# Sigmoid attention into a swish MoE layer: values loaded ahead of group 2, group 0's values between the first half visits, keys cast and turned tile by tile

## Chip, cores, metric

The kernel runs on 1 core of one Trainium2 chip. The metric is device time in microseconds (us); less is better. A core has TensorE (PE, its weight loads shown as PEld), VectorE (DVE), ScalarE (ACT), GpSimd (POOL) and SyncE (SP); POOL and SP issue DMAs here.

## What is computed

```python
scores = q @ k.transpose(0, 1, 3, 2) / sqrt(64) - log(448)      # 8 batches, 12 heads, 448 x 64
attn_out = sigmoid(scores) @ v
x = attn_out.transpose(0, 2, 1, 3).reshape(8 * 448, 12 * 64)    # 3584 x 768
h = x @ w_in                                                     # 768 x 2048
out = (h * sigmoid(beta * h)) @ w_out                            # 2048 x 768
```

Inputs and output are float32; the kernel works in float16 with float32 sums.

## The kernel before

Heads are taken four at a time: a **group** `g` holds the queries and keys of 4 heads of a batch, with 32 partitions for each head, and a batch has 3 groups (`QPB`). A group has two **slots** of 2 heads. 448 keys are three tiles of 128 (`JF` = 3) and a last tile of 64.

Loads go through POOL's queue (`load_one` L111, `load_v` L132, `load_w_in` L151, `load_w_out` L158) and cast float32 to float16 on the way. Only what is needed first goes another way: half of group 0's queries and all its keys are brought in as float32 by SP (L723, "staged" in a piece of `gt`) and cast by ACT and DVE (L747 to L750). `transpose` (L191) turns queries and keys 32 by 32 on DVE; keys of a group take one instruction for the three full tiles (L204) and one for the last (L208). `load_v` brings the full tiles with four DMAs (L136) and the last tile with two (L143); `double_v_last` (L145) copies the last tile's values to a second half of the partitions, on DVE.

`score` (L215) is a matmul of a key tile with queries into a PSUM score tile; `weigh` (L227) is the sigmoid on ACT that reads it (L230). For the start of batch 0 there are three score tiles and two further PSUM banks (L711), and the work is cut into **half visits** (`half_visit`, L256): half of the queries (224) of a group, first with key tiles 0 and 1, then with tile 2 and the last. Each uses two score tiles and ends in two ACT instructions. `attend` (L279) multiplies the weights with v into two PSUM banks (L291), which DVE copies to `xT` (L300). Then the first layer starts: `first_half(n)` makes n `dense1` (L305) of six matmuls on `w_in` each (L171, through the helper `dense`).

All of this is in an order written by hand (`tc.manual_schedule`, L713): each engine takes its instructions in the order of the program. From L713 to L809 the order is written out; behind it `follow(STEPS)` (L810) goes through a long list. The order around the change, before:

1. SP stages; PE runs 11 matmuls on zeros (`idle_units`, L738, L744); group 0's queries and keys are cast and turned.
2. POOL issues, in this order: half the queries and the keys of groups 1 and 2, v of batch 0 (6 DMAs), late queries of groups 0 and 1, `w_in` in 8 pieces, with group 2's late queries between.
3. Six half visits (groups 0, 1, 2, early queries), with 4, 4, 4, 4 and 2 idle units behind the first five (L767 to L771).
4. `double_v_last(0)`, group 0's late queries, `attend(0)`, half visit, `attend(1)`, half visit (L772 to L777), then the others' late queries, `attend(2)` in two parts, and the turning of beta.
5. The score tiles go from three to two, and the first layer starts (L794 to L796); its first matmul waits for the last ACT of the half visits.

The DMA semaphores of POOL are eight in turn; an issue waits for the landing of the eighth issue before it.

Of the kernel before, what the change touches and what calls it, by code (L numbers as in the profile page):

```python
# [8 lines left out]
FP32 = mybir.dt.float32  # L9
FP16 = mybir.dt.float16  # L10
# [3 lines left out]
def kernel(  # L14
# [10 lines left out]
    nc = tc.nc  # L25
# [82 lines left out]
    raws = {}  # L108
# [20 lines left out]
    def last_base(s: int) -> int:  # L129
        return (s % 2 ^ swapped(s // 2)) * KL  # L130

    def load_v(b: int):  # L132
        vs[b] = vp.tile([P, H, JF + 1, D], FP16, tag="v16", name="v16")
        rows = v[b].rearrange("h (p c) d -> p h (c d)", c=NB)
        for i in range(HQ):
            nc.gpsimd.dma_start(  # L136
                out=vs[b][i * BLK : (i + 1) * BLK, :, 0:JF].rearrange("p h j d -> p h (j d)"),
                in_=rows[:, :, JF * i * D : JF * (i + 1) * D],
            )
        rows = v[b].rearrange("h (p c) d -> p h c d", c=NB)  # L140
        for c in range(NF, NB):
            lo = (c - NF) * BLK
            nc.gpsimd.dma_start(out=vs[b][lo : lo + BLK, :, JF], in_=rows[:, :, c])  # L143

    def double_v_last(b: int):  # L145
        nc.vector.tensor_copy(out=vs[b][KL:P, :, JF], in_=vs[b][0:KL, :, JF])
# [44 lines left out]
    def transpose(g: int, r: int, c0: int = 0, c1: int = NB):  # L191
        raw = raws[g][:, r]
        if r == 0:
            if g not in qT:
                qT[g] = qTp.tile([P, NB * BLK, PAIR], FP16, tag="qT", name="qT")
            nc.vector.transpose(
                out=in_order(g // QPB, qT[g][:, c0 * BLK : c1 * BLK]),
                in_=raw[:, c0:c1].rearrange("p c d -> p (c d)").bitcast(FP32),
            )
            return  # L200
        kT[g] = kTp.tile([P, S, PAIR], FP16, tag="kT", name="kT")
        to = kT[g].rearrange("p k e -> p (k e)").bitcast(FP32)
        frm = raw.rearrange("p c d -> p (c d)").bitcast(FP32).rearrange("p (c f) -> p c f", c=NB)
        nc.vector.transpose(  # L204
            out=to[:, 0 : JF * P].rearrange("p (j i q) -> p i j q", j=JF, i=HQ),
            in_=frm[:, 0:NF].rearrange("p (i j) f -> p i j f", j=JF),
        )
        nc.vector.transpose(  # L208
            out=to[:, JF * P :], in_=frm[:, NF:].rearrange("p c f -> p (c f)")
        )  # L210
# [502 lines left out]
    with tc.manual_schedule():  # L713
        raws[0] = rawp.tile([P, 2, NB, D], FP16, tag="raw", name="raw")
        wide = gt.rearrange("p a b -> p (a b)").bitcast(FP32)
        cut = NH * D
        early = [(0, 0, NH), (1, 0, NB)]
        staged = {}
        at = 0
        for r, c0, c1 in early:  # L720
            staged[r] = wide[:, at : at + (c1 - c0) * D]
            at += (c1 - c0) * D
            nc.sync.dma_start(  # L723
                out=staged[r],
                in_=(q, k)[r][0, 0:HQ].rearrange("h (p c) d -> (h p) (c d)", c=NB)[
                    :, c0 * D : c1 * D
                ],
            )
        nc.gpsimd.memset(dummy, 0.0)
        nc.scalar.activation(out=dummy, in_=dummy, func=AF.Sigmoid, bias=0.0, scale=1.0)  # L730

        still = gt[:, NDC - 1, 0:512]
        nc.vector.memset(still, 0.0)
        beta_in = sigp.tile([P, S], FP32, tag="sg", name="beta_in")[0:BLK, 0:P]
        nc.vector.memset(beta_in, 0.0)
        idle = bank("idle_ps", 512)

        def idle_units(n: int, cols: int = 512):  # L738
            for _ in range(n):
                nc.tensor.matmul(  # L740
                    idle[:, 0:cols], still[:, 0:P], still[:, 0:cols], start=True, stop=True
                )

        idle_units(10)  # L744
        idle_units(1, 256)
        raw = raws[0].rearrange("p r c d -> p r (c d)")
        nc.vector.tensor_copy(out=raw[:, 0, 0:cut], in_=staged[0])  # L747
        transpose(0, 0, 0, NH)
        nc.scalar.copy(out=raw[:, 1, cut:], in_=staged[1][:, cut:])  # L749
        nc.vector.tensor_copy(out=raw[:, 1, 0:cut], in_=staged[1][:, 0:cut])  # L750
        transpose(0, 1)
        for g in range(1, QPB):
            load_one(g, 0, 0, NH)
            load_one(g, 1)
        load_v(0)
        nc.sync.dma_start(out=beta_in[0:NDC], in_=moe_beta.rearrange("(c p) -> c p", p=P))
        for g in range(QPB - 1):
            load_one(g, 0, NH, NB)
        for c in range(WCH):
            if c == WCH // 2:  # L760
                load_one(QPB - 1, 0, NH, NB)
            load_w_in(c)
        for g in range(1, QPB):
            transpose(g, 0, 0, NH)
            transpose(g, 1)

        for g in range(QPB):  # L767
            for second in range(2):
                half_visit(g, 0, second)
                if 2 * g + second < 2 * QPB - 1:  # L770
                    idle_units(4 if g < QPB - 1 else 2)  # L771
        double_v_last(0)  # L772
        transpose(0, 0, NH, NB)
        attend(0, 0, QH)
        half_visit(0, QH, 0)
        attend(1, 0, QH)
        half_visit(0, QH, 1)  # L777
        for g in range(1, QPB - 1):
            transpose(g, 0, NH, NB)
        attend(2, 0, QH, (0,))  # L780
        attend(2, 0, QH, (1,))
        for i in range(P // BLK):
            part = slice(i * BLK, (i + 1) * BLK)
            nc.vector.transpose(out=beta_sb[part], in_=beta_in[:, part])
# [24 lines left out]
        first_half(1)  # L809
        follow(STEPS)  # L810
# [30 lines left out]
```

## Time and profile before

| | |
|---|---|
| median of 3 runs | 368.48 us (368.26 to 369.42) |
| the profiled execution | 368.51 us, its span 366.7 us, granted clock 1.0 |
| busy: PE / DVE / ACT / POOL | 361.6 / 271.7 / 248.7 / 154.3 us |
| stretch 0 to 6.00 us, PE busy | 4.67 (idle matmuls on zeros) |
| 6.00 to 13.08, PE / ACT busy | 7.08 / 6.13 |
| 13.08 to 19.42, PE / ACT busy | 5.95 / 6.14 |
| 19.42 to 34.50, PE / ACT busy | 15.08 / 11.89 |
| moved by DMA in these four stretches | 166, 179, 184, 201 GB/s |

The profile is of one execution on the chip, times from the start of its span. A timeline line gives start, length, engine, line of the kernel, operation, what is written and read with shape and type, how many were merged, and in brackets how long the engine had been idle and what ended that. A line of the chain gives start, length and who held the chain. A line of the DMA issues gives what is written and read, queue, count, KB each and the time from issue to landing.

### The profile page before, as it was taken

Reading aid. Unit: us, or ns where it says so; the run is one execution under the profiler, and the core shown is the slowest. Engines: PE = TensorE matmul, PEld = TensorE weight load, DVE = VectorE, ACT = ScalarE, POOL = GpSimd, SP = SyncE. Lnnn points to the kernel's source line nnn. Section 1 sums busy time; section 2 is a strip of 40 time slices with the busy share of each in tenths; the row PEclk is TensorE's granted clock in tenths of the full one; section 3 lists DMA queues with packets and bytes.
Section 4 is the critical chain, followed back from the end, with each engine's and each line's share of the span. In section 5 each row is a group of like instructions: output and inputs, shape, how many; then the busy total and the mean of one; then the engine's idle time right before and its main releaser. Section 6 shows DMA issues by size and latency. Waiting matters only on the chain.

```text
span 366.7 us, 9126 instructions
## 1 busy us (share of the span) xinstructions
PE 361.6 (99%) x3677; PEld 238.0 (65%) x3677; DVE 271.7 (74%) x521; ACT 248.7 (68%) x409; POOL 154.3 (42%) x192
## 2 busy tenths in 40 slices
PE   8999999999999999999999999999999999999996
PEld 3478754457465685557857667666856687679763
DVE  3356569889995796876778678868878667678764
ACT  4987976789765797657865579977874859226410
POOL 7834523504413873117761445841630316316610
PEclk9999999999999999999999999999999999999999
DMA  8999999930363790416919363373303030030234
GB/s 168 184 197 201 199 206 198 236 39 2 50 139 52 160 152 2 74 64 111 156 13 149 52 137 52 49 81 89 52 1 89 2 88 2 0 88 0 56 68 138
DMA packets 42698, 34.76 MB, mean 95 GB/s; under 512 B 21904, under 2 KB 39200, under 8 KB 42656
## 3 DMA queue, kind: packets, MB, share of 16 engines
q0 software_dynamic: 36688, 22.47, 44.8%
q1 hardware_dynamic: 5968, 11.71, 11.5%
q8 instruction: 29, 0.48, 0.6%
q14 instruction: 13, 0.11, 0.1%
HBM read 45.62 MB, written 11.01 MB: 154 GB/s over the span
## 4 chain that ended last, share of the span: by engine, by line
PE 93%; DMA 3%; ACT 2%; DVE 1%; SPq 0%; issue 0%; ACTq 0%; DVEq 0%
PE m_ps L171 71%; PE sco L218 12%; PE av_ps L291 9%; DMA out_dram<-osb 2%; ACT attnT L230 1%; PE idle_ps L740 1%; DMA gt<-in_k_dram 1%; DVE osb L372 0%; SPq L602 0%; ACT osb L425 0%; DVE xT L300 0%; DVE kT L204 0%; ACT raw L749 0%; ACT osb L463 0%; SPq L723 0%
## 5 line engine op out<-in xcount | busy, mean ns | idle before, releaser
L230 ACT ACTIVATE attnT<-sco 128x896 f16<-128x896 f32 (+1 forms) x163 | 139.2, 908 | 37.8 <-PE sco L218 37.1
L372 DVE TENSOR_TENSOR osb<-m_ps,osb 128x448 f32<-128x448 f32 (+2 forms) x197 | 116.3, 596 | 51.1 <-PE m_ps L171 42.0
L171 PEld LDWEIGHTS <-w_in 128*128 128x128 f16 (+1 forms) x948 | 81.0, 100 | 18.8 <-issue 11.0
L171 PE MATMUL m_ps<-xT,w_in 128*128 128x224 f16 (+3 forms) x750 | 85.5, 266 | 0.3 <-ACT attnT L230 0.2
L492 POOL TENSOR_TENSOR gt<-osb,sg 128x448 f16<-128x448 f32 x26 | 29.5, 1135 | 117.8 <-ACT sg L425 107.7
L502 POOL TENSOR_TENSOR gt<-osb,sg 128x448 f16<-128x448 f32 x52 | 58.3, 1138 | 35.1 <-ACT sg L425 33.5
L425 ACT ACTIVATE sg<-osb,beta_sb 128x224 f32<-128x224 f32 (+1 forms) x104 | 54.0, 575 | 10.3 <-DVE osb L372 10.0
L171 PEld LDWEIGHTS <-sum 128*128 128x128 f16 (+1 forms) x444 | 39.9, 99 | 27.4 <-issue 3.6
L171 PEld LDWEIGHTS <-gt 128*128 128x128 f16 (+1 forms) x474 | 36.9, 102 | 25.7 <-issue 7.5
L171 PE MATMUL m_ps<-w_out,gt 128*128 128x384 f16 (+2 forms) x350 | 52.6, 324 | 0.0
L218 PE MATMUL sco<-qT,kT 32*128 32x448 f16 (+3 forms) x864 | 51.5, 340 | 0.3 <-ACT attnT L230 0.2
L171 PEld LDWEIGHTS <-w_S 128*128 128x128 f16 (+1 forms) x486 | 43.9, 99 | 7.0 <-issue 6.0
L171 PE MATMUL m_ps<-w_out,sum 128*128 128x384 f16 (+1 forms) x228 | 40.6, 327 | 0.0
L171 PE MATMUL m_ps<-w_T,sum 128*128 128x384 f16 (+1 forms) x216 | 40.3, 326 | 0.0
L300 DVE CAST xT<-av_ps 128x448 f16<-128x448 f32 (+1 forms) x54 | 28.4, 566 | 14.2 <-PE av_ps L291 14.1
L291 PE MATMUL av_ps<-attnT,v 128*64 128x448 f16 (+3 forms) x400 | 38.2, 343 | 0.0
L171 PE MATMUL m_ps<-xs,w_S 128*128 128x224 f16 (+1 forms) x330 | 36.2, 259 | 0.0
L291 PEld LDWEIGHTS <-v 128*64 128x64 f16 (+1 forms) x432 | 20.4, 108 | 17.7 <-issue 9.8
L425 ACT ACTIVATE osb<-m_ps,beta_sb 128x224 f32<-128x224 f32 x52 | 20.4, 448 | 15.4 <-PE m_ps L171 15.1
L218 PEld LDWEIGHTS <-kT 32*128 32x128 f16 (+1 forms) x864 | 13.5, 96 | 23.1 <-issue 21.5
L320 DVE TENSOR_TENSOR gt<-m_ps,sg 128x224 f16<-128x224 f32 (+1 forms) x40 | 16.6, 434 | 12.5 <-ACT sg L317 12.2
L463 ACT COPY osb<-m_ps 128x448 f32<-128x448 f32 x26 | 13.8, 535 | 17.7 <-PE m_ps L171 15.5
(50 smaller groups left out, 303.5 us busy)
## 6 DMA issues: line engine op xcount, KB each, us to landing
out_dram<-osb SPq DMA_DIRECT2D x100, 96.0 KB, 2.4
raw<-in_k_dram POOLq DMA_DIRECT2D x23, 224.0 KB, 5.7
raw<-in_q_dram POOLq DMA_DIRECT2D x21, 224.0 KB, 4.4
v<-in_v_dram POOLq DMA_DIRECT2D x32, 144.0 KB, 7.0
w_in<-in_moe_w_in_dram POOLq DMA_DIRECT2D x8, 384.0 KB, 10.3
w_out<-in_moe_w_out_dram POOLq DMA_DIRECT2D x4, 768.0 KB, 13.1
v<-in_v_dram POOLq DMA_DIRECT2D x16, 48.0 KB, 6.4
out_dram<-osb SPq DMA_DIRECT2D x4, 192.0 KB, 2.4
```

Source lines behind the costliest of these rows:

```text
L171: nc.tensor.matmul(to[c : c + step], hidden[:, c : c + step], weights, **({} if step == P else {"tile_position": (0, c)}), **flags,)
L218: nc.tensor.matmul(sco[base : base + nk, hh, u0 : u0 + n], kT[g][lo : lo + BLK, jt * P : jt * P + nk, e], qT[g][lo : lo + BLK, c0 : c0 + n ...
L230: nc.scalar.activation(out=at[:, :, 0:n], in_=sco[:, :, 0:n], func=AF.Sigmoid, bias=NEG_LOG_S, scale=MSCALE,)
L291: nc.tensor.matmul(av[hh * D : (hh + 1) * D, 0:n], vs[b][base : base + nk, 2 * (s % NPAIR) + hh, jt], at[base : base + nk, hh, 0:n], start ...
L300: nc.vector.tensor_copy(out=xTs[b][:, s % NPAIR, c0 : c0 + n], in_=av[:, 0:n])
L320: nc.vector.tensor_tensor(out=gt[:, dc, off : off + n], in0=m1[:, 0:n], in1=sg[:, 0:n], op=ALU.mult)
L372: nc.vector.tensor_tensor(out=out, in0=in0, in1=in1, op=op)
L425: nc.scalar.activation(out=out, in_=in_, func=AF.Sigmoid, bias=0.0, scale=beta_sb[:, dc : dc + 1])
L463: nc.scalar.copy(out=oa[:, 0], in_=m)
L492: nc.gpsimd.tensor_tensor(out=gt[:, 2 * d : 2 * d + 2, off : off + QH], in0=ob[:, 0], in1=sg, op=ALU.mult)
L502: nc.gpsimd.tensor_tensor(out=gt[:, dc, off : off + S].rearrange("p (h n) -> p h n", h=2), in0=oa[:, :, j], in1=sg, op=ALU.mult,)
L740: nc.tensor.matmul(idle[:, 0:cols], still[:, 0:P], still[:, 0:cols], start=True, stop=True)
```

## The change

Three things, all in the hand-written start. `load_v` is split into `load_v_full` (the full tiles, of some heads) and `load_v_last` (the last tile, all heads); for batch 0 the last tile of all heads and the full tiles of heads 0 to 3 (group 0's) are issued between group 1's and group 2's queries and keys, and heads 4 to 11 behind them: 10 DMAs instead of 6. Group 0's keys are cast by tile (tile 1 and the last on ACT, tiles 0 and 2 on DVE) and turned by tile. `double_v_last(0)` and `attend(0)` go between the half visits of the early queries, `attend(1)` ahead of group 0's late half visits, and the idle units become 3, 4, 4, 4, 0, 1, with 10 instead of 11 at the start; each call of `idle_units` takes a bank of its own.

```diff
+    def load_v_full(b: int, h0: int, h1: int):
+        rows = v[b, h0:h1].rearrange("h (p c) d -> p h (c d)", c=NB)
         for i in range(HQ):
             nc.gpsimd.dma_start(
-                out=vs[b][i * BLK : (i + 1) * BLK, :, 0:JF].rearrange("p h j d -> p h (j d)"),
+                out=vs[b][i * BLK : (i + 1) * BLK, h0:h1, 0:JF].rearrange("p h j d -> p h (j d)"),
                 in_=rows[:, :, JF * i * D : JF * (i + 1) * D],
             )
+
+    def load_v_last(b: int):
         rows = v[b].rearrange("h (p c) d -> p h c d", c=NB)
         for c in range(NF, NB):
             lo = (c - NF) * BLK
             nc.gpsimd.dma_start(out=vs[b][lo : lo + BLK, :, JF], in_=rows[:, :, c])
...
-        idle_units(10)
+        idle_units(9)
         idle_units(1, 256)
...
-        nc.scalar.copy(out=raw[:, 1, cut:], in_=staged[1][:, cut:])
-        nc.vector.tensor_copy(out=raw[:, 1, 0:cut], in_=staged[1][:, 0:cut])
-        transpose(0, 1)
+        whole = [
+            t[:, 0 : NF * D].rearrange("p (i j d) -> p i j d", j=JF, d=D)
+            for t in (staged[1], raw[:, 1])
+        ]
...
+        def key_cast(copy, j: int):
+            copy(out=whole[1][:, :, j], in_=whole[0][:, :, j])
+
+        def key_turn(j: int):
+            nc.vector.transpose(
+                out=words[:, j * P : (j + 1) * P].rearrange("p (i q) -> p i q", i=HQ),
+                in_=raws[0][:, 1, 0:NF]
+                .rearrange("p c d -> p (c d)")
+                .bitcast(FP32)
+                .rearrange("p (i j q) -> p i j q", i=HQ, j=JF)[:, :, j],
+            )
+
+        key_cast(nc.scalar.copy, 1)
+        nc.scalar.copy(out=raw[:, 1, NF * D :], in_=staged[1][:, NF * D :])
+        key_cast(nc.vector.tensor_copy, 0)
+        key_turn(0)
+        key_turn(1)
+        key_cast(nc.vector.tensor_copy, 2)
+        key_turn(2)
+        nc.vector.transpose(out=words[:, JF * P :], in_=raw[:, 1, NF * D :].bitcast(FP32))
...
         for g in range(1, QPB):
             load_one(g, 0, 0, NH)
             load_one(g, 1)
-        load_v(0)
+            if g == 1:
+                load_v_last(0)
+                load_v_full(0, 0, HQ)
+        load_v_full(0, HQ, H)
...
-        for g in range(QPB):
-            for second in range(2):
-                half_visit(g, 0, second)
-                if 2 * g + second < 2 * QPB - 1:
-                    idle_units(4 if g < QPB - 1 else 2)
         double_v_last(0)
+        for n in range(2 * QPB):
+            half_visit(n // 2, 0, n % 2)
+            if n == 2 * QPB - 2:
+                attend(0, 0, QH)
+            else:
+                idle_units((3, 4, 4, 4, 0, 1)[n])
         transpose(0, 0, NH, NB)
-        attend(0, 0, QH)
+        attend(1, 0, QH)
         half_visit(0, QH, 0)
-        attend(1, 0, QH)
         half_visit(0, QH, 1)
```

More of the change, by code (lines that the diff above doesn't have):

```diff
@@ L130, in last_base @@
         return (s % 2 ^ swapped(s // 2)) * KL
-    def load_v(b: int):
-        vs[b] = vp.tile([P, H, JF + 1, D], FP16, tag="v16", name="v16")
-        rows = v[b].rearrange("h (p c) d -> p h (c d)", c=NB)
+    def load_v_full(b: int, h0: int, h1: int):
+        rows = v[b, h0:h1].rearrange("h (p c) d -> p h (c d)", c=NB)
         for i in range(HQ):
             nc.gpsimd.dma_start(
-                out=vs[b][i * BLK : (i + 1) * BLK, :, 0:JF].rearrange("p h j d -> p h (j d)"),
+                out=vs[b][i * BLK : (i + 1) * BLK, h0:h1, 0:JF].rearrange("p h j d -> p h (j d)"),
                 in_=rows[:, :, JF * i * D : JF * (i + 1) * D],
             )
+    def load_v_last(b: int):
         rows = v[b].rearrange("h (p c) d -> p h c d", c=NB)
@@ L143, in load_v @@
             nc.gpsimd.dma_start(out=vs[b][lo : lo + BLK, :, JF], in_=rows[:, :, c])
+    def load_v(b: int):
+        vs[b] = vp.tile([P, H, JF + 1, D], FP16, tag="v16", name="v16")
+        load_v_full(b, 0, H)
+        load_v_last(b)
     def double_v_last(b: int):
@@ L735 @@
         nc.vector.memset(beta_in, 0.0)
-        idle = bank("idle_ps", 512)
         def idle_units(n: int, cols: int = 512):
+            idle = bank("idle_ps", 512)
             for _ in range(n):
@@ L748 @@
         transpose(0, 0, 0, NH)
-        nc.scalar.copy(out=raw[:, 1, cut:], in_=staged[1][:, cut:])
-        nc.vector.tensor_copy(out=raw[:, 1, 0:cut], in_=staged[1][:, 0:cut])
-        transpose(0, 1)
+        whole = [
+            t[:, 0 : NF * D].rearrange("p (i j d) -> p i j d", j=JF, d=D)
+            for t in (staged[1], raw[:, 1])
+        ]
+        kT[0] = kTp.tile([P, S, PAIR], FP16, tag="kT", name="kT")
+        words = kT[0].rearrange("p k e -> p (k e)").bitcast(FP32)
+        def key_cast(copy, j: int):
[16 more added lines that the diff above has]
+        nc.vector.transpose(out=words[:, JF * P :], in_=raw[:, 1, NF * D :].bitcast(FP32))
+        vs[0] = vp.tile([P, H, JF + 1, D], FP16, tag="v16", name="v16")
         for g in range(1, QPB):
```

## The prediction

> **What bounds the kernel now.** I read the page first: its span, the shares of the engines and the chain that ended last.
>
> ```profile
> span 366.7 us, 9126 instructions
> PE 361.6 (99%) x3677; PEld 238.0 (65%) x3677; DVE 271.7 (74%) x521; ACT 248.7 (68%) x409; POOL 154.3 (42%) x192
> PE 93%; DMA 3%; ACT 2%; DVE 1%; SPq 0%; issue 0%; ACTq 0%; DVEq 0%
> ```
>
> PE is the bound almost everywhere, and behind 19.42 us every engine has the same instructions in the same order in both kernels. So the change is worth what it moves the first dense matmul at 19.42, as far as the stage behind it can follow. That stage I read in the chain in order of time, up to that matmul:
>
> ```profile
> 1.18 3.56 DMA gt<-in_k_dram
> ...
> 6.00 0.62 PE sco L218 x16
> ...
> 16.29 3.08 ACT attnT L230 x4
> ...
> 19.42 2.46 PE m_ps L171 x24
> ```
>
> Columns are start, length, who. The staged keys land at 4.74, are cast and turned, PE scores at 6.00, and the dense stage starts when the last ACT of the block ends. Whether ACT or PE sets the pace in between I read from ACT's timeline:
>
> ```profile
> 6.66 6.28 ACT L230 ACTIVATE early<-sco 128x896 f16<-128x896 f32 x8 [1.33 <-PE sco L218]
> 13.08 6.29 ACT L230 ACTIVATE attnT<-sco 128x896 f16<-128x896 f32 x8
> 20.49 1.87 ACT L317 ACTIVATE sg<-m_ps,beta_sb 128x224 f32<-128x224 f32 x4 [1.12 <-DVE beta_sb L784]
> ```
>
> Sixteen sigmoids run from 6.66 to 19.37 with 0.14 between the eights: 12.71 us. Asked in narrow windows they start at 6.66, 7.47, 8.37, ..., 16.29, 17.11, 18.01. With three score tiles the second tile of a half visit waits for the ACT two back, and that half visit's last matmul starts the ACT after: third = end of the first (7.57) + 0.8 = 8.37; thirteenth = end of the eleventh (15.71) + 0.58 = 16.29. So the block is a **locked chain of PE and ACT**: it moves as a whole with its first ACT, and the idle matmuls only fill PE's waits. DVE's timeline gives the keys:
>
> ```profile
> 4.76 0.39 DVE L750 CAST raw<-gt 128x448 f16<-128x448 f32 x1 [0.51 <-DMA gt<-in_k_dram]
> 5.36 0.58 DVE L204 STREAM_TRANSPOSE kT<-raw 128x384 f32<-128x384 f32 x1 [0.20 <-ACT raw L749]
> 5.86 0.20 DVE L208 STREAM_TRANSPOSE kT<-raw 128x64 f32<-128x64 f32 x1
> 7.46 0.58 DVE L204 STREAM_TRANSPOSE kT<-raw 128x384 f32<-128x384 f32 x1 [1.10 <-DMA raw<-in_k_dram]
> 9.18 0.58 DVE L204 STREAM_TRANSPOSE kT<-raw 128x384 f32<-128x384 f32 x1 [0.67 <-DMA raw<-in_k_dram]
> 14.15 0.35 DVE L146 COPY v<-v 64x768 f16<-64x768 f16 x1 [4.27 <-DMA v<-in_v_dram]
> ```
>
> Group 1's keys land at about 7.43, group 2's at 9.15, the last of v at 14.06: DVE waits on each.
>
> **Keys tile by tile: gain 0.43.** Now the scores wait for a whole ACT half (0.57) and a turn of 384 (0.58). In the changed list the first turn of 128 waits for DVE's cast of tile 0 and also for ACT's cast of tile 1, though it reads tile 0 alone. That ACT copy has 256 columns instead of 448. ACT rows: 0.56 for 448, 0.45 for a 224-column sigmoid, so about 0.45. The turn: 0.20 for 64, 0.58 for 384, on the line between them 0.28 for 128. Turn starts 4.76+0.45+0.03 = 5.24, ends 5.52, PE starts 5.57 (0.05 later, as 5.94 to 6.00) instead of 6.00: 0.43. Bounds: cast 0.45 to 0.57 and turn 0.20 to 0.41 (the 224 row) give 0.18 to 0.51; should the stride slow both casts, nothing is gained, and that is the lower end. Turn 1 ends at 5.72, ahead of the ninth matmul (5.57+0.25). Tile 2 and the tail end by 6.45, while the second half visit comes at 6.85; ACT's extra copy (128 columns) ends by 5.6, ahead of the first sigmoid at 6.23. Two extra turns and a cast on DVE lie before group 1's keys (7.43). They cost nothing on that cover; without it, some 0.3.
>
> **PE's clock: loss 0.1.** The eleven idle matmuls before 6.00 take 4.66, starting 0.43 apart; those at 6.55 take 1.04 for four, 0.22 apart. PE changes from half to full speed at about 6. Scores that start at 5.57 fall partly into the slow time; whole it would cost 0.58 (the undisturbed sixteen at 21.81 take 0.58, at half speed twice that), for the first third of it I take 0.1, 0 to 0.58. The Trainium skill ("TensorE: Matmul & The Clock Gate", Part 1) says the gate opens after a busy window of about 3.4 us that runs freely, so that the switch differs from run to run. One trace can't show that; by it the cost varies between executions and isn't fixed at 6.
>
> **attend(0) between the half visits, attend(1) ahead of the next: loss 0.2.** Of the 29 idle units 26 stay. attend(0) takes 0.91 (14.67 to 15.58, next weight load). Between first and second half visit of group 2 PE has 13.06 to 14.05, of which 0.5 are idle units: it fits, no loss. Between the second and the next score PE had exactly attend(0), 0.91; now one idle unit (0.24) and attend(1) (0.91): 1.15. So the thirteenth ACT comes 0.2 later than its lock, and the last with it. Afterwards PE has nothing between two half visits, 0.7 idle, and both parts of attend(2) come late as before, 0.92 in all, done before the last ACT. Bounds 0 to 0.35 (should the idle unit wait out both DVE casts, 0.69 from the end of attend(0), it is still covered by the 0.7 of scores between).
>
> **v ahead of group 2's queries and keys: nothing lost, barely.** Ahead go two transfers of 48 KB for the last keys and four of 48 KB: 288 KB. The 16 engines move 179 GB/s in 6.00 to 13.08, so 1.65 us. Group 2's keys then land at 9.15+1.65 = 10.8, up to 11.4 if v's last rows lag (landing 12.71 to 14.06 for 96 KB: 1.35 where 0.55 is the rate). They are turned 0.63 later: 11.4 to 12.05. The half visit wants them at 12.43-0.43 = 12.0. Issue: POOL has eight landings outstanding at most: its tenth issue, now one of v, waits for the second to land, group 1's keys.
>
> ```profile
> 7.72 0.61 POOL L143 DMA_DIRECT2D v<-in_v_dram  x1 [1.07 <-DMA raw<-in_k_dram]
> ```
>
>  So group 2's keys are issued at 7.72 instead of 3.03. In this row from issue to landing
>
> ```profile
> raw<-in_k_dram POOLq DMA_DIRECT2D x1, 224.0 KB, 6.1
> ```
>
> most is queueing; in a quiet time (94 us) the same takes 4.2, and as large a transfer with nothing ahead of it (93 us) 3.7: landing by 11.4 then. Cost 0 to 0.05, at the row's 6.1 far more (rival). POOL issues four more DMAs, 0.62 each = 2.5, so the weights of the first layer are issued near 12 instead of 10.29; queued bytes cover that, as w_in's first chunk takes 6.2 to land, its own 2.0 included. The doubling copy stands on DVE behind group 2's turn and takes 0.35 (to 12.4); attend(0) needs it only for its last four matmuls after 12.6. Group 0's late queries, 14.54 now, are wanted at 15.4.
> The Trainium skill ("DMA: Bandwidth & Descriptors", Rules for kernel authors) says to join transfers, as under 64 KB one pays mostly overhead; it speaks against this cut. Here queued transfers of v of 144 KB and of 48 KB follow each other by 0.85 and 0.36, so the trace bears it out little: behind others overhead is hidden. With the fixed cost of about 2.0 us that the page gives (Anatomy of one DMA), an estimate by that page alone is 6 x 2.0 = 12 us more if nothing overlapped, keys at 21.
>
> **Sum.** 0.43 - 0.1 - 0.2 = 0.13 of gain at 19.42. Behind it PE can follow: the w_in chunks land at least 0.5 ahead of their first matmul (last at 31.50 for 32.09), w_out 0.6 (43.62 for 44.21). The profiled execution took 368.51 (span 366.7, 1.8 around it), beside a median of 368.48: 368.51-0.13 = **368.4**. With all good ends 0.51: 368.0; with all bad ones (0, 0.58, 0.35): 369.4.
>
> **Rivals.**
> 1. Group 2's keys come late (slower). For it: issued 4.69 later, behind a landing; all data of this time were waited for. Against: the rate. With the queued 6.1, landing is 13.85, the half visit starts 14.5 instead of 12.0: 368.4+2.5 = 370.9. It decides from a landing beyond 11.4, and from about 12.6 the kernel is over 0.3% slower. Chance 0.14. The Trainium skill's rule on small transfers stands on this side.
> 2. PE's clock opens late, after the first scores and three idle units: 0.58 and 3 x 0.21, less the idle unit that was dropped (0.22): 1.0 lost, 369.3. For: the scores start earlier. Against: 4.4 us of idle matmuls lie before, and before is open to the same. Chance 0.10.
> 3. The gain is real, but w_in lands later by the four issues, and PE waits there instead: 368.5 to 368.9 (0.5 late at the chunks with 0.5 to spare). For: the page's slices stay near 200 GB/s up to 73 us. Against: same bytes. Chance 0.10.
> 4. What no row shows: 0.07, of which 0.04 faster.
>
> My forecast has 0.59. **Chances:** within 0.3% (about 1.1 us, what a measurement of this kernel can tell from no change) 0.59+0.10+0.10 = 0.79; slower 0.14+0.03 = 0.17; faster 0.04, as no case reaches it. Range 367.8 to 369.6: forecast and rivals 2 and 3, and the first part of 1.
>
> **What would show it.** First score at about 5.57; its first ACT 6.23; group 2's first half visit at 12.0 without a wait for DVE or keys; a PE gap of 0.7 before the last half visit of the block; first dense matmul at 19.3; no PE wait for w_in. I am wrong if group 2's turn waits beyond 11.4, if the first turn starts before ACT's cast ends, or if idle matmuls 0.43 apart stand behind the first scores.

## The result, and the profile after

| | before | after |
|---|---|---|
| median, measured side by side | 368.69 us (368.11 to 371.01, 7 runs) | 370.50 us (370.12 to 372.49, 7 runs) |
| profiled execution, span | 368.51, 366.7 | 370.74, 368.8 |

The ratio is 1.0051, 95% interval 1.0029 to 1.0073: slower by about 1.8 us, where 368.4 was forecast. The page of after, the lines that answer to those of before:

```profile
PE 360.9 (98%) x3674; PEld 237.2 (64%) x3674; DVE 272.4 (74%) x524; ACT 249.0 (68%) x410; POOL 156.2 (42%) x196
...
PE 86%; DMA 10%; POOL 2%; issue 1%; DVE 0%; ACT 0%; DVEq 0%; POOLq 0%
```

PE does the same work (360.9), but transfers now hold 10% of the chain instead of 3%, and POOL, which was not on it, 2%. Where they stand shows the chain in order of time, cut at 60 us (start, length, who):

```profile
1.98 5.30 DMA raw<-in_k_dram
...
7.56 0.55 POOL raw L115
...
13.13 9.55 DMA w_in<-in_moe_w_in_dram
22.97 12.85 DMA raw<-in_k_dram
...
36.94 8.98 DMA w_out<-in_moe_w_out_dram
```

The chain no longer goes through the scores. It goes from the landing of group 1's keys to POOL, which issues group 2's keys only then, through POOL's issues to the third piece of the first layer's weights, whose landing at 22.69 lets POOL issue again, and so on to the weights of the second layer, which land at 45.92. So up to there the chain runs through POOL's eight places. PE's timeline around 22 to 25 us, before and then after:

```profile
22.32 1.90 PE L171 MATMUL m_ps<-xT,w_in 128*128 128x224 f16 x18
```

```profile
22.73 1.32 PE L177 MATMUL m_ps<-xT,w_in 128*128 128x224 f16 x12
24.74 0.46 PE L177 MATMUL m_ps<-xT,w_in 128*128 128x224 f16 x3 [0.68 <-DMA w_in<-in_moe_w_in_dram]
```

PE waits 0.68 for the fourth piece of the weights, a wait that the forecast said would not be there. ACT's timeline has the block of half visits (6.10 to 19.61 us):

```profile
6.10 6.28 ACT L236 ACTIVATE early<-sco 128x896 f16<-128x896 f32 x8 [0.82 <-PE sco L224]
12.77 3.06 ACT L236 ACTIVATE attnT<-sco 128x896 f16<-128x896 f32 x4 [0.40 <-PE sco L224]
16.54 3.07 ACT L236 ACTIVATE attnT<-sco 128x896 f16<-128x896 f32 x4 [0.70 <-PE sco L224]
```

ACT has the same instructions in both kernels behind 6 us, so one can set the two traces beside each other instruction by instruction. After minus before: -0.56 at the first sigmoid, -0.31 at the ninth, +0.25 at the thirteenth (16.54 for 16.29), then flat until the first layer; +0.83 and +1.15 at the two instructions that before started at 24.69 and 25.02 (the waits for the weights), +1.74 at the one of 46.56 (the second layer's weights), and between +1.75 and +2.02 from 103 on, +2.01 at the last. Of the 2.23 between the two profiled executions the block of half visits has 0.25, the first layer's weights 0.90, the second layer's 0.6. The last step of 0.27 and the 0.2 that lie outside this comparison were not followed up.

Last, DVE's timeline of after, then POOL's timeline of before and of after, which show where the lateness begins:

```profile
5.12 0.51 DVE L766 STREAM_TRANSPOSE kT<-raw 128x128 f32<-128x128 f32 x2
...
11.53 0.58 DVE L210 STREAM_TRANSPOSE kT<-raw 128x384 f32<-128x384 f32 x1 [1.72 <-DMA raw<-in_k_dram]
```

```profile
10.29 3.53 POOL L153 DMA_DIRECT2D w_in<-in_moe_w_in_dram  x4 [0.30 <-DMA v<-in_v_dram]
```

```profile
3.74 2.15 POOL L135 DMA_DIRECT2D v<-in_v_dram  x4
...
7.56 0.55 POOL L115 DMA_DIRECT2D raw<-in_k_dram  x1 [1.12 <-DMA raw<-in_k_dram]
8.10 2.32 POOL L135 DMA_DIRECT2D v<-in_v_dram  x4
...
11.49 3.33 POOL L159 DMA_DIRECT2D w_in<-in_moe_w_in_dram  x4
```

POOL's tenth issue waits for the second to land, as the forecast said, and the weights are issued at 11.49 instead of 10.29, as it said (near 12). What it did not say is how little was left in the queue on the way there. At 7.6 us POOL had issued 1296 KB in before (112 and 224 KB for each of groups 1 and 2, four times 144, once 48) and 736 KB in after (112, 224, six times 48, 112); some 560 KB had moved in either. So 740 KB were ahead of the engines before, 180 KB after: 1.0 us of work at the 179 GB/s of the forecast. Two stretches, after and then before (the last column is GB/s, the one before it the DMA share):

```profile
8.00:10.00 2.00, 2.00 (x24) 0.84 (x22) 0.42 (x2) 1.85 (x3) 2.00 (x5) 1.00 0.93 110
...
14.00:16.00 2.00, 1.76 (x34) 0.98 (x33) 0.79 (x3) 1.84 (x3) 2.00 (x3) 1.00 1.08 140
```

```profile
8.00:10.00 2.00, 2.00 (x29) 0.91 (x30) 1.21 (x5) 1.85 (x4) 1.44 (x3) 1.00 1.42 176
...
14.00:16.00 2.00, 1.95 (x44) 1.23 (x45) 1.07 (x3) 2.00 (x3) 2.00 (x3) 1.00 1.44 189
```

By 16 us after had moved 332 KB less, 1.8 us of full rate. What POOL has issued cannot move at once: in E10, below, it took 2.7 us from an issue into empty engines to the full rate. Counted with these 2.7 us, an estimate, at each full microsecond from 8 to 14 no more than 130 KB were ready and waiting in after, and never under 137 in before. By 14 us 237 of the 332 KB were lost. At 15 us after had 376 KB ready and still moved 140 GB/s in the next one, before 185, so a short queue does not explain the rest.

The first packets of the weights began to move at 14.42 instead of 12.93, so the 1.20 by which they were issued later came through whole and grew. The eight pieces of the first layer's weights landed from 18.66 instead of 16.52, the second layer's first piece at 45.92 instead of 43.62, all 1.5 to 2.3 us late.

### The profile page after: what moved, and what is told of

Read it like the earlier page. It is cut to its first block, busy times and chain, and to the rows that moved or that the text cites. A ratio compares the mean times of both kernels' runs of the same rounds, so it can differ in the third digit from the quotient of the medians.

```text
span 368.8 us, 9130 instructions
## 1 busy us (share of the span) xinstructions
PE 360.9 (98%) x3674; PEld 237.2 (64%) x3674; DVE 272.4 (74%) x524; ACT 249.0 (68%) x410; POOL 156.2 (42%) x196
## 4 chain that ended last, share of the span: by engine, by line
PE 86%; DMA 10%; POOL 2%; issue 1%; DVE 0%; ACT 0%; DVEq 0%; POOLq 0%
PE m_ps L177 68%; PE sco L224 10%; PE av_ps L297 8%; DMA raw<-in_k_dram 5%; DMA w_in<-in_moe_w_in_dram 3%; DMA w_out<-in_moe_w_out_dram 2%; POOL raw L115 1%; POOL v L135 1%; DVE osb L378 0%; POOL w_in L159 0%; ACT attnT L236 0%; POOL v L144 0%; ACT osb L469 0%; POOL dummy L735 0%; DVEq L378 0%
## 5 line engine op out<-in xcount | busy, mean ns | idle before, releaser
L498 POOL TENSOR_TENSOR gt<-osb,sg 128x448 f16<-128x448 f32 x26 | 29.5, 1135 | 118.1 <-ACT sg L431 107.7
L177 PEld LDWEIGHTS <-gt 128*128 128x128 f16 (+1 forms) x474 | 36.9, 102 | 26.2 <-issue 8.1
L135 POOL DMA_DIRECT2D v<-in_v_dram x36 | 21.8, 615 | 12.5 <-DMA w_out<-in_moe_w_out_dram 6.5
## 6 DMA issues: line engine op xcount, KB each, us to landing
w_in<-in_moe_w_in_dram POOLq DMA_DIRECT2D x8, 384.0 KB, 11.4
```

Source lines behind the costliest of these rows:

```text
L135: nc.gpsimd.dma_start(out=vs[b][i * BLK : (i + 1) * BLK, h0:h1, 0:JF].rearrange("p h j d -> p h (j d)"), in_=rows[:, :, JF * i * D : JF * ...
L177: nc.tensor.matmul(to[c : c + step], hidden[:, c : c + step], weights, **({} if step == P else {"tile_position": (0, c)}), **flags,)
L498: nc.gpsimd.tensor_tensor(out=gt[:, 2 * d : 2 * d + 2, off : off + QH], in0=ob[:, 0], in1=sg, op=ALU.mult)
```

## The experiments

The theory after the result is a **supply theory**: POOL may have eight transfers outstanding, each takes it about 0.55 us to issue (0.83 for a piece of weights), so what lies ahead of the engines is counted in transfers. Four more small ones leave too few bytes ahead, the engines run dry, and everything behind comes late. The rivals: the *place* of the moved loads, a cost of each transfer or cut by itself (the *count*), or one of the other two parts of the change.

All medians stand beside runs of before on the same chip (368.36 to 368.74 in the four groups of runs). "Weights" is the landing of the first, second and fourth piece of `w_in` in the profiled execution.

| kernel | median | ratio to before (95%) | weights |
|---|---|---|---|
| before | 368.69 | | 16.52, 18.51, 22.57 |
| after | 370.50 | 1.0051 (1.0029 to 1.0073) | 18.66, 20.70, 24.69 |
| E1 keys alone | 368.68 | 0.9995 (0.9982 to 1.0008) | 17.15, 19.14, 23.16 |
| E2 loads alone | 370.39 | 1.0057 (1.0035 to 1.0079) | 18.63, 21.02, 25.03 |
| E3 order alone | 370.19 | 1.0045 (1.0027 to 1.0063) | 17.06, 19.06, 23.05 |
| E4 after, group 2 ahead of the full tiles | 371.51 | 1.0074 (1.0051 to 1.0097) | 18.98, 20.96, 26.32 |
| E5 cut in the old place | 372.00 | 1.0109 (1.0084 to 1.0133) | 20.40, 22.36, 26.42 |
| E6 moved, not cut | 369.62 | 1.0031 (1.0019 to 1.0042) | 17.36, 19.12, 23.14 |
| E7 last keys' v moved, not cut | 368.82 | 1.0008 (0.9998 to 1.0018) | 17.01, 19.00, 23.02 |
| E8 E2 with weights between | 374.55 | 1.0159 (1.0136 to 1.0181) | 15.25, 20.78, 24.78 |
| E9 four empties among v | 372.61 | 1.0113 (1.0089 to 1.0137) | 20.32, 22.71, 26.77 |
| E10 four empties ahead of the weights | 372.19 | 1.0095 (1.0074 to 1.0116) | 18.54, 21.45, 25.91 |
| E11 two of four cut | 369.75 | 1.0025 (1.0014 to 1.0037) | 17.36, 19.52, 23.55 |
| E12 E7 with the new keys | 368.49 | 0.9998 (0.9986 to 1.0009) | 16.41, 18.41, 22.43 |
| E13 E3 again, one execution | 369.14 | | 16.18, 18.17, 22.19 |
| E14 E12 with the new order | 369.90 | 1.0036 (1.0019 to 1.0053) | 16.88, 18.77, 22.75 |
| E15 four empties behind the second piece | 369.55 | 1.0029 (1.0017 to 1.0040) | 15.88, 17.91, 23.16 |

### E1 to E3: each part of the change by itself

E1 is before with the casts and turns of the change and ten idle matmuls ahead instead of eleven; E2 is before with the split `load_v` and this list; E3 is before with the new order of half visits, attends and idle units. In these and most kernels below each call of `idle_units` also takes a bank of its own, as in after.

```diff
+        vs[0] = vp.tile([P, H, JF + 1, D], FP16, tag="v16", name="v16")
         for g in range(1, QPB):
             load_one(g, 0, 0, NH)
             load_one(g, 1)
-        load_v(0)
+            if g == 1:
+                load_v_last(0)
+                load_v_full(0, 0, HQ)
+        load_v_full(0, HQ, H)
```

> Before with the keys cast and turned tile by tile alone (and 9 instead of 10 whole idle units at the start); loads and order of before. Supply theory (the changed kernel is slower because POOL's queue of transfers runs dry at 8.5 to 16 us, so that w_in and all behind it land 2 us later than before): supply is as before here, the first score comes at 5.5, the first dense matmul 0.4 to 0.5 earlier than 19.42, and the w_in chunks with 0.5 to spare just let that pass: 368.0 to 368.4, 0.3 to 0.5 under before. Rival order theory (the loss is made in the block by attend(0) and attend(1) between the half visits): the same gain. Rival that the keys' cut itself costs: at or above before.

> Before with the loads of the change alone: v's last tile and heads 0 to 3 ahead of group 2's queries and keys, heads 4 to 11 behind; keys and order of before. Supply theory: group 2's keys land at 11.5, in time for 12.43, the block ends as before at 19.4, but the first w_in chunk lands near 18.7 and the others 1.5 to 2.2 later than before; PE waits at the second and third chunk and at w_out, 1.8 to 2.3 us in all: 370.3 to 370.8. Order theory: no loss, 368.5.

> Before with the order of the change alone: attend(0) between the half visits of group 2, attend(1) ahead of group 0's late half visits, fewer idle units; keys and loads of before, v's last tile landing at 14.06. Supply theory: w_in lands as before; attend(0) waits for the doubling copy of v, to 14.5 instead of 13.1, and the block ends 1.2 to 1.6 later, near 20.8; PE's waits are all in the block: 369.6 to 370.2. Order theory as it stands (the loss is the place of the attends, not the wait for v): 370.5, with the block's end as late as 21.5.

E2 makes the whole loss of the change: 370.39. PE waits for the weights (0.71 for the fourth piece), and the weights land as late as in after (18.63). The block did not end as before, as had been expected: PE waited 0.43 for group 0's late queries, and the dense stage started at 19.93 instead of 19.42. E1 missed its 368.0 to 368.4. It brings the first score forward by 0.38 and the dense stage by 0.12 in the profiled execution (5.62, 19.30), since its first sixteen scores took 0.88 instead of 0.62, and PE then waits 0.47 for the sixth piece: nothing is left at the end. E3 by itself loses 1.1 to 2.5 in five of its six executions, while the profiled one (368.72) shows only 0.3 at the dense start; a second profiled execution is in E13. The losses of the parts do not add up: 0.3, 2.0 and 1.8 alone, 1.8 together. In before's loads the new order waits for v (E13), which the moved loads bring earlier.

### E4: group 2's keys ahead of the full tiles, cut kept

```diff
-        for g in range(1, QPB):
-            load_one(g, 0, 0, NH)
-            load_one(g, 1)
-            if g == 1:
-                load_v_last(0)
-                load_v_full(0, 0, HQ)
+        load_one(1, 0, 0, NH)
+        load_one(1, 1)
+        load_v_last(0)
+        load_one(2, 0, 0, NH)
+        load_one(2, 1)
+        load_v_full(0, 0, HQ)
         load_v_full(0, HQ, H)
```

> The changed kernel with one step moved: the two transfers of v's last tile stay ahead of group 2's queries and keys, the four of heads 0 to 3 go behind them. No issue up to the eighth waits for a landing, so group 2's keys are issued near 4.3 instead of 7.56. Supply theory: no gap in the transfers at 8.5 to 10, group 2's keys at about 9.8, w_in's first chunk at most 1.2 later than before (what is left are four more issues); 368.3 to 369.4. Order theory: the block's order is the changed kernel's, so 370.5 stays.

A miss: 371.51. Group 2's keys were issued at 4.47 and landed at 9.75, so the late issue of these keys was mended, and the gap at 8.5 to 10 was gone; but from 9.5 to 18 the engines moved 117 to 161 GB/s in stretches of 1 us, with eight transfers of 48 and 96 KB in a row, v landed at 15.13 and the weights at 18.98. Mending one transfer's issue moves the hole behind it. It is the cut, not the wait of that one transfer. In the profiled execution (372.33, while three of the six took 370.2 to 370.8) PE waited 2.04 for the fourth piece, and the granted clock was 0.5 from 26.2 to 29.5.

### E5 to E7: cut or place

E5 leaves v behind group 2 and only cuts it (the last tile comes between the two parts); E6 moves v ahead of group 2 without cutting; E7 moves only its two last tiles, uncut. All three have before's keys and order.

```diff
 E5
-        load_v(0)
+        load_v_full(0, 0, HQ)
+        load_v_last(0)
+        load_v_full(0, HQ, H)
...
 E6 (E7 has the last line behind group 2's)
         load_one(1, 0, 0, NH)
         load_one(1, 1)
+        load_v_last(0)
+        load_v_full(0, 0, H)
         load_one(2, 0, 0, NH)
         load_one(2, 1)
```

> The kernel before (its keys, its order of half visits and attends) with the transfers of v cut as in the changed kernel, ten instead of six, but left behind group 2's queries and keys: nothing is moved. Lead theory (POOL may have eight landings outstanding; four smaller transfers more mean that fewer bytes are issued ahead, the engines run dry, and everything behind lands later): group 2's keys land at 9.2 as before, the weights of the first layer are issued 1 to 1.5 later and their first piece lands at 17.5 to 18 instead of 16.5, PE waits for them 0.5 to 1.5 in all, run 369.2 to 370.2. Position theory (the loss is made by the place of group 2's keys alone): first piece of the weights at 16.5, run 368.4.

> The kernel before with v moved ahead of group 2's queries and keys, but uncut: all heads, six transfers, the same in number and size as before. Lead theory: group 2's keys are issued behind group 1's landing and land at 12.5 to 13.4, the block of half visits moves by about 1, but the bytes issued ahead stay large, so the weights land within 0.5 of before; the loss is that of the late keys less what the weights' slack absorbs: 369.0 to 369.8, with no or little wait of PE for the weights. Position theory: weights' first piece lands at 18 or later, and PE waits for it at least 1.5 as with the loads of the changed kernel alone, 370.4.

> The kernel before with only the two transfers of v's last keys moved ahead of group 2's queries and keys; six transfers of the same sizes. Lead theory: group 2's keys land 0.5 later (9.7) with 2 to spare, the bytes issued ahead are the same, the weights' first piece lands at 16.5 to 16.8, run 368.4. Position theory: as the place of group 2's keys changes by two transfers of the six, a part of the loss, 369.

E5 alone, with nothing moved, costs more than the whole change: 372.00, above what either theory gave. The place theory is out. E6 pays for the place as worked out (group 2's keys land at 13.15, PE waits 1.00 for them, 369.62), without a wait for weights. E7 costs nothing that can be told from before. E5's stretches are lower for longer than after's:

```profile
10.00:12.00 2.00, 2.00 (x23) 0.73 (x24) 0.51 (x3) 2.00 (x3) 2.00 (x4) 1.00 1.13 111
12.00:14.00 2.00, 1.93 (x23) 0.69 (x22) 0.00 (x0) 1.85 (x4) 2.00 (x4) 1.00 1.15 128
```

The columns are the length, busy time and count of PE, PEld, DVE, ACT and POOL, granted clock, DMA share and GB/s. POOL is busy 2.00 of 2.00: it does nothing but issue, 96 KB in each 0.57 us, 172 GB/s where the engines of before moved 190, and before that it had waited twice for a landing (1.50 until 7.89, 0.64 until 9.71). Counted with E10's 2.7 us as above, no more than 33 KB were ready at any full microsecond from 10 to 15. Low rates went on to 20 us (134 and 151 GB/s) with 290 KB ready at 16 and 1180 at 18, which a short queue does not explain.

### E8: a large piece between

> The loads of the changed kernel on the kernel before (by themselves 370.4), but with the first piece of the first layer's weights, a large transfer, issued behind group 2's keys and ahead of the four transfers of heads 4 to 11. Lead theory: the queue runs dry at 8.5 to 10 as with the changed loads, but not again at 11 to 16; the weights' later pieces land 0.5 to 1 behind those of the kernel before instead of 2, run 368.8 to 369.4; v's heads 4 to 11 come 1.2 later, at 15 to 15.5, just in time or 0.3 late. Rival (the low rate from 11 on has another cause than what is issued): the second low stretch stays and PE waits for the weights' second and third piece as before, 370.4.

```diff
+        load_w_in(0)
         load_v_full(0, HQ, H)
...
-            load_w_in(c)
+            if c:
+                load_w_in(c)
```

Inconclusive on its question, and a miss: 374.55. The piece of 384 KB pushed the landing of group 0's late queries from 15.44 in after to 18.21, which the expectation had left out:

```profile
18.70 0.93 PE L224 MATMUL sco<-qT,kT 32*128 32x224 f16 x16 [2.83 <-DVE qT L202]
```

PE waited 2.83 and then ran its next two half visits in 0.93 and 1.07 instead of 0.58 to 0.74: the granted clock was 0.5 from 17.4 to 27.6. A long wait of PE in this stage can cost twice, once as a wait and once as a slower clock. In E4 and E9 it was 0.5 for 3.4 us, with waits of 2.04 and 1.13; behind waits of 1.00 (E6) and 1.15 (E10) it stayed at 1.0.

### E9, E10, E15: four transfers that carry nothing

The same four transfers of 32 bytes into a tile that nobody reads, in before's kernel, at three places: one ahead of each full tile of v (E9), ahead of the first piece of `w_in` (E10), behind its second piece (E15).

```diff
+        for i in range(HQ):
+            nc.gpsimd.dma_start(out=empties[i : i + 1, 0:8], in_=moe_beta[8 * i : 8 * i + 8].rearrange("(o n) -> o n", o=1))
         for c in range(WCH):
```

> The kernel before with four transfers of 32 bytes put on POOL's list, one ahead of each of the four uncut transfers of v: the number of transfers is that of the cut, the bytes and sizes of all others are those of before. Nothing reads the four. Supply theory (what costs is that the engines run out of issued bytes, not the number of transfers): POOL issues the weights at about 11.7, the engines are busy with v until 13.8, so they do not run dry, the weights' first piece lands at 16.5 to 17.3, run 368.4 to 369.2. Count theory (each transfer costs by itself): first piece at 18 or later, run 370 or more.

> The kernel before with the same four transfers of 32 bytes put just ahead of the weights of the first layer: only the weights' issue is later, by some 2.2 (12.5 instead of 10.3), which the prediction held to be covered by queued bytes. If they cover it: first piece of the weights at 16.5, run 368.4. Supply theory by arithmetic (a transfer's first bytes move about 1.9 after its issue starts, as measured where the engines were idle): the engines wait from 13.8 to 14.4, first piece at 17.1 to 17.3, PE waits 0.1 to 0.4, run 368.5 to 369.0. If running dry also slows the engines for some microseconds behind it, as it looks in the kernels with the cut: first piece at 18 or later, run 370 or more.

> The kernel before with the same four transfers of 32 bytes, now behind the second piece of the first layer's weights instead of just ahead of the first one. Supply theory: the two pieces hold the engines until 18, the third is issued near 14.4 and moves from 16.3 on, so nothing runs dry: pieces land at 16.5, 18.5, 20.6, 22.6 as before, run 368.4 to 368.9. Count theory: four transfers more cost what they cost ahead of the first piece, 370 to 372.

128 bytes in all cost 3.6 us ahead of the weights and 0.8 us behind the second piece: **place in the queue decides, neither bytes nor count alone.** E10 is the prediction's own step laid bare, since nothing but the issue of the weights is moved, though by more than in the change (3.2 instead of 1.2). POOL's timeline:

```profile
11.07 0.51 POOL L769 DMA_DIRECT2D empties<-in_moe_beta_dram  x1 [0.25 <-DMA v<-in_v_dram]
...
12.78 0.50 POOL L769 DMA_DIRECT2D empties<-in_moe_beta_dram  x1 [0.42 <-DMA v<-in_v_dram]
13.51 3.33 POOL L159 DMA_DIRECT2D w_in<-in_moe_w_in_dram  x4 [0.24 <-DMA v<-in_v_dram]
```

An empty transfer takes one of the eight places as long as a full one, so each issue waits for a landing of v: the weights leave 3.2 later, not 4 times 0.5. The engines had finished their queue at about 14; between 14 and 16 they moved 21 GB/s:

```profile
14.00:16.00 2.00, 1.84 (x39) 1.11 (x42) 0.56 (x2) 2.00 (x4) 2.00 (x4) 1.00 0.23 21
```

and PE waits for the weights' second, third and fourth piece, longest for the fourth:

```profile
25.96 0.75 PE L177 MATMUL m_ps<-xT,w_in 128*128 128x224 f16 x6 [1.15 <-DMA w_in<-in_moe_w_in_dram]
```

In E15 the two pieces ahead cover the four: the same stretch moves 197 GB/s, and PE does not wait for the first layer's weights at all. E15 is still 0.8 over before, above the 0.5 that the supply theory allowed, and below the count theory's 370 to 372. Two things are in it. Each empty transfer held each engine for 0.2 us although it was queued (the middle one of the 16 engines completed the piece ahead at 17.20 and the four at 17.38, 17.57, 17.75 and 17.91), 0.7 for four. And in the profiled execution all but 0.1 of its loss comes at the second layer's weights: PE waits 0.6 at 45.16, which the profile puts down to DVE; but DVE's instruction had long been done, and the weights landed at 45.02. Fifteen of the 16 engines had finished them by 43.67, one at 45.02. So up to 0.8 of what four more transfers cost may be their number alone; what lies above that is their place.

E9 did not run as expected (372.61 against at most 369.2). The expectation counted the issues at 0.55 each and forgot that the ninth and later ones wait: the last full tile of v was issued at 9.88, the weights at 12.80, and from 10 to 16 the engines moved 86, 113 and 134 GB/s (2 us each). The last of v also landed at 15.79 instead of 14.06, PE waited 1.13 for it in the block, and the dense stage started at 21.42, so that E9 tells less of the weights than E10. By itself E9 is what the count theory said (370 or more); E15, with the same four, is not.

### E11: half of the cut

```diff
-        load_v(0)
+        for i, h0, h1 in ((0, 0, HQ), (1, 0, HQ), (2, 0, H), (3, 0, H), (0, HQ, H), (1, HQ, H)):
+            nc.gpsimd.dma_start(
+                out=vs[0][i * BLK : (i + 1) * BLK, h0:h1, 0:JF].rearrange("p h j d -> p h (j d)"),
+                in_=rows0[:, h0:h1, JF * i * D : JF * (i + 1) * D],
+            )
+        load_v_last(0)
```

> The kernel before with v in its old place behind group 2, two of its four large transfers cut into heads 0 to 3 and 4 to 11, two left whole: eight transfers instead of six or ten. With all four cut in this place the run took 372.0 and the first piece of the weights landed at 20.4. Supply theory: fewer bytes are missing, the engines run dry for a third or less as long, first piece of the weights at 17 to 18.5, run 368.8 to 370.2. If the cut of a transfer by itself costs, each the same: half of the loss, 370.2.

Eight transfers instead of ten: 369.75, a third of E5's loss (1.1 of 3.6), first piece at 17.36. That fits a queue that runs dry for a shorter time; a fixed price for each cut would give half (370.2), outside the interval.

### E12 to E14: the rest of the change once the loads are as before

E12 has the keys of after, the order of before and the loads of E7; E13 is E3; E14 is E12 with the order of after.

```diff
 E14 against after
         load_one(1, 0, 0, NH)
         load_one(1, 1)
         load_v_last(0)
-        load_v_full(0, 0, HQ)
         load_one(2, 0, 0, NH)
         load_one(2, 1)
-        load_v_full(0, HQ, H)
+        load_v_full(0, 0, H)
```

> The candidate that these findings point to: keys cast and turned tile by tile as in the changed kernel, the order of half visits of the kernel before, v uncut, and only the two transfers of v's last keys ahead of group 2's. Theory: dense stage starts 0.1 to 0.4 earlier than 19.42, but the weights land no earlier than before and PE waits for them, as with the keys alone: run 368.2 to 368.7. Rival: the gain at the start reaches the end, run 368.0 or less.

> The kernel with only the order of half visits and attends changed (median 370.19, 368.72 to 370.88, the profiled execution 368.72), a second execution with a profile. If the loss is a wait of the earlier attends for v, which lands behind group 2's keys: the attend between the half visits waits longer than the 1.44 that it took, the dense stage starts at 20 or later, run 369.5 to 370.9. If the loss is in the transfers: PE waits for the weights by 1 or more, dense stage near 19.7.

> The changed kernel with its keys and its order, v uncut and of its transfers only those of the last keys ahead of group 2's; so the attend between the half visits asks for v while it lands (13.1 to 13.5). Theory: the weights land as before (16.4 to 17.0), PE does not wait for them by more than 0.3, the block loses 0.5 to 1 at v instead: run 368.6 to 369.8. If the order costs nothing by itself: 368.4 or less. If the order costs what it cost alone: 370.2.

E12 is the best version that the findings point to: new keys, old order, v uncut with its last tiles ahead of group 2. Its profiled execution is the shortest of all (367.85, span 366.0, dense stage at 18.67), with the whole of the block 0.74 earlier and 0.2 given back at a piece of weights; 0.27 of the 0.74 are the staged keys, which landed at 4.47 instead of 4.74 in this execution. Its median, 368.49, cannot be told from before (0.9986 to 1.0009). E13, the order alone in a second profiled execution (369.14, below the 369.5 expected), answers E3:

```profile
13.82 0.65 PE L297 MATMUL av_ps<-early,v 64*64 64x224 f16 x4 [0.26 <-DMA v<-in_v_dram]
```

The attend that now lies between the half visits waits for v, whose last part lands at 13.68 in before's order of loads; the dense stage starts at 20.04, 0.62 later than in before, and stays so to the end. The five slower executions of E3 lost more than this (1.1 to 2.5), and none of them has a trace. E14 (order and keys, v uncut) is the same: 0.87 of waiting for v, dense stage at 20.37, no wait for weights, 369.90 (0.1 above what was expected). So the order asks for v earlier, and getting it earlier by the cut costs the weights. Either way the change pays.

## Why the prediction was wrong, point by point

- **Keys tile by tile (0.43) and the clock (0.1 lost): the gain right, the rest luck.** The first turn waited for ACT's cast of tile 1 as said (DVE's cast ends at 4.98, ACT's at 5.09, the turn starts at 5.12). From the landing of the staged keys to the first score it took 1.26 in before (4.74 to 6.00) and 0.83 in after (4.66 to 5.49), in E1, E12 and E14 too: 0.43 less, as forecast. The first sigmoid came 0.56 earlier instead of 0.33, as the keys landed 0.08 earlier and the clock cost nothing in this execution: the first sixteen scores took 0.58. In E1 sixteen scores took 0.88, in E15 0.94 at an old start of 5.81: the clock's opening varies between executions, and the bounds of 0 to 0.58 hold it. The Trainium skill ("TensorE: Matmul & The Clock Gate", Part 1) says that the window in which PE's work is judged runs freely; these three starts agree.
- **Group 2's keys (nothing lost, barely): nearly right.** Landing 11.50 for 10.8 to 11.4, from issue to landing 3.9 as estimated from quiet times, 0.25 lost for at most 0.05. The turn started at 11.53, past the 11.4 that the prediction had named as a sign of being wrong, but the loss of rival 1 (2.5) did not follow.
- **Order of the attends: right in kind, too small.** 0.2 was forecast; it cost 0.56 (from -0.31 to +0.25), of which 0.24 was a wait of `attend(1)` for the last of v, which the step had not asked about. In E14's loads `attend(0)` waits 0.87 for v.
- **The step that failed: "POOL issues four more DMAs, 0.62 each = 2.5, so the weights of the first layer are issued near 12 instead of 10.29; queued bytes cover that".** The issue time was near (11.49; 10.29 and 2.5 would be 12.8). The cover, which put the lateness at nothing, was wrong: the weights began to move 1.49 later and landed 2.14 later, and PE lost 0.90 at them and 0.6 at the second layer's. The cover was taken from before, where the engines were never without work (740 KB ahead at 7.6 us), and not worked out again for a list of smaller transfers, where it was 180 KB. The engines moved 94 GB/s from 8.5 to 10 and 140 to 161 from 10 to 16. E10 shows that a late issue of the weights costs by itself once the queue is empty (3.6 us for 3.2), and E2 that the loads alone make the loss. Of the 332 KB that were missing at 16 us, 237 had been lost by 14 us with a short queue; what cost the other 95 is open. The two slack figures of the sum (0.5 at `w_in`, 0.6 at `w_out`) were right, and 2 us of lateness went through both.
- **Rival 3 named the mechanism** (weights later by the four issues, PE waits) and sized it at 0.5, with "same bytes" against it. The bytes are the same; when they are issued is not. With the deficit that was then measured its price is 332 KB by 16 us, 1.8 us, less the slack of 0.5 at the weights, plus the 0.25 of the block: about 1.6, measured 1.8.
- **The Trainium skill's rule** ("DMA: Bandwidth & Descriptors", Rules for kernel authors) to join small transfers spoke against the change and was right in its sign. The prediction set it aside because transfers of 48 KB followed each other by 0.36. That row was true and still is: what a queued transfer costs the engines is little (0.2 us for an empty one, E15). The rest of the price lies in the issuing engine's list, where each transfer costs a place out of eight.

What stays open: the engines were slow for longer than the missing issues explain. In E10 the first piece of weights finished at 18.35 on the middle engine; the second, issued at 14.35, took 2.7 behind it, and in E5 3.1, while in E7 and E12 it took 2.0. But in before and in E1, whose queues had not run dry, it took 2.4 and 2.5, so that a dry spell is not shown to be what makes the next one slow. The Trainium skill ("SBUF — State Buffer", the trap it calls "DVE blocks DMA") offers that POOL cannot write its transfers' descriptors while DVE runs certain instructions. E5 moved 128 GB/s from 12 to 14 with DVE at 0.00 busy, where POOL's issues explain it, and E10 moved 25 GB/s from 15.50 to 15.75, a hole behind the first packets of the weights, with DVE idle since 14.36. No run here separates DVE from the later stretches. It was not settled.

## What to carry to other kernels

A queue that allows so many transfers outstanding has its lead in *transfers*: bytes ahead = places times the size of what fills them. Before cutting or adding transfers on the list that also issues the next stage's weights, work out for the moment of their issue how many microseconds of bytes are ahead of the engines (here eight places, 0.55 us an issue, and in E10 1.6 us from the issue at 13.51 to the first bytes and 2.7 to the full rate), and compare that with the slack of every load behind. Only what was issued that long ago counts as ahead. A load moved earlier is paid for by what it moves past, and the bill can come two stages later.

## What the runs showed of the hardware

- Four transfers of 32 bytes each made a kernel of 368 us slower by 3.6 us (E10) or by 0.8 us (E15), by their place on POOL's list alone.
- The landing of a transfer is that of the slowest of 16 engines, and the lag of the slowest can stay for as long as the queue is full: in E1 fourteen engines finished the fifth, sixth and seventh piece of weights by 25.20, 27.20 and 29.20, the last one at 26.56, 28.60 and 30.57. In each kernel the profile has packets of 16 KB on the instruction queue, 0.9 to 1.3 us each up to 50 us, in before at 13.07, 23.33, 31.63 and 42.67, in E1 at 23.35. That these are what holds one engine back fits in time and size, and is argued, not shown; it would account for a part of the spread between executions.
- Small packets are not slow when queued: in before, v's packets of 384 and of 128 bytes moved at 174 to 185 GB/s between 9 and 12 us, the weights' of 512 bytes at 195 to 199 from 18 to 21.
